# Mixing the first two token tiles side by side, chunk by chunk, with three tiles of token weights turned between them

## The chip, the cores and the metric

The kernel runs on one core of a Trainium2 chip. Its time is the device time of one execution in microseconds (us). Several executions are made, and the median counts. One further execution is taken by the hardware profiler; its times carry line numbers (L419 is line 419 of the kernel before). Engines are called PE (matmul), PEld (its weight load), DVE (vector), ACT (scalar), POOL (GpSimd) and SP (which issues DMAs here).

## The reference

Two blocks follow each other, for a batch of 4, 8 heads, 768 tokens (S) and a head size of 64 (so 512 channels):

```python
scores = scale * q @ k.T + bias            # bias falls off with distance, one slope per head
keep   = is_global | is_local              # 8 global keys, and the last 96 positions
x      = softmax(where(keep, scores, -1e9)) @ v      # -> [B, S, 512]

theta = x @ w_theta
zr, zi = x * cos(theta), x * sin(theta)
y = einsum('ts,bsd->btd', w_tok_r, zr) + einsum('ts,bsd->btd', w_tok_i, zi)
u = x + y
out = u + maximum(u @ w_ch, 0)
```

Inputs and output are float32; the kernel computes in bf16 with float32 sums.

## The kernel before, in words

Tokens are cut into 6 tiles of 128 (NT), channels into 4 (NC), heads into 4 pairs (NP). The loop runs over the batches `b` = 0 to 3. For each batch there are these steps, each a small function:

- **Preparation** (`prep`, batches 1 and 2): DVE copies a head pair's queries and keys into `qkn` (L231, two copies a pair), PE turns them (L246), DVE copies the turned queries to `qT` (L250) and ACT the turned keys to `kT` (L252); `kglob` makes `kG` from `kT` with two DVE copies (L220, L222). Batch 3 is turned by DMA transposes instead (`prep_dma`, L263).
- **Scores** (`scores`): a pair `p` has three chunks `c`. Matmuls go into a wide PSUM buffer `pb` (L296), ACT takes the exponential into `e` (L306), DVE multiplies with a table (L315, L318).
- **Values** (`values`, L355): `e` times `vn` into a wide PSUM buffer; DVE divides by the row sums (`rec`, L364) into `x_sb` (L366). From batch 1 on, `xtrans` turns `x_sb` into `xT` by a DMA transpose that SP issues (L370).
- **Theta** (`theta`, L398): `xT` times `w_theta` in three chunks `c` of two token tiles; ACT takes cosine and sine into `cs` (L404), DVE multiplies with `x_sb` into `zri` (L408). `theta(b, c, 1)` and `(b, c, 3)` complete a chunk and issue its sines.
- **Mix** (`mix(b, tt, g)`, L419): output tile `tt` gets 12 matmuls, 4 for each chunk `g` of two source tiles (cosine and sine part by turns), into one small PSUM tile; after the last, DVE adds `x_sb` to give `u` (L424).
- **`trans_w(tt)`** turns the two token weight matrices for output tile `tt`: 6 PE transposes each into a small PSUM tile (L167), one copy each into `w_tokT` (L168). The copy of the second can be given to ACT. This is done once, for batch 0.
- **`utrans`** turns `u` into `uT` (PE and an ACT copy, L437 and L438, for batch 0; a DMA transpose, L433, afterwards), and **`chan`** multiplies it with `w_ch` (L447), adds and stores (L452, L454).

PSUM has two pools: `big`, two buffers of two banks each (tag `pb`, for scores, for values from batch 1 on, and for theta's first two chunks), and `small`, four buffers (tag `ps`, for all else).

The order has two regimes. All of batch 0 up to its last sine is written out by hand and kept as written (`manual_schedule`); there theta's chunk 0, 1 and 2 are followed by nothing but the tables of `bias_table(1..7)` on ACT. After that a scheduler orders the instructions of each engine ahead of time, and each engine then runs its list in order. What it is given is a list that `weave` makes: `main` (the mixes of batch `b`, with `trans_w`, `chan` and `utrans` among them) and `side` (the attention of batch `b + 1` and preparations), each step with a weight; `weave` spreads `side` between a start share and 0.9 of `main`. For batch 0 the start share is 0.3. Some instructions are fixed behind others (`behind`, `issue_after`).

Loads go over POOL's queue in program order: after the first pieces of batch 0 come the weights, then queries and keys of batch 1, `vn` of batch 1, queries and keys of batch 2, `vn` of batch 2 (its buffer is set by a DVE memset first, L68), half of the queries and keys of batch 3 (L82, into the buffer of batch 1's, so behind the `qkn` copies). The rest of batch 3's loads stand behind `gate` (L469), a one-element POOL copy from `xT` of batch 1, pair 3.

The old order of the mix, and of the weights in `main`:

```python
        for st in (2 * g, 2 * g + 1):
            for wi in range(2):
                anchor["pe"] = nc.tensor.matmul(
...
                if b == 0 and g == 1 and tt + 1 < NT:
                    main.append((1536, lambda tt=tt: trans_w(tt + 1, nc.scalar.copy if tt > 1 else nc.vector.tensor_copy)))
```

Of the kernel before, what the change touches and what calls it, by code (L numbers as in the profile page):

```python
# [9 lines left out]
FP = mybir.dt.float32  # L10
BF = mybir.dt.bfloat16
AF = mybir.ActivationFunctionType
# [4 lines left out]
def kernel(  # L17
# [13 lines left out]
    nc = tc.nc  # L31
    B, H, S, D = q.shape
    T = 128
    NT = S // T
    DM = H * D
    NC = DM // T
    NP = H // 2
# [11 lines left out]
    moe = ctx.enter_context(tc.tile_pool(name="moe", bufs=2))  # L49
    big = ctx.enter_context(tc.tile_pool(name="big", bufs=2, space=bass.MemoryType.PSUM))  # L50
    small = ctx.enter_context(tc.tile_pool(name="small", bufs=4, space=bass.MemoryType.PSUM))

    def ps_big():
        return big.tile([T, 2, 512], FP, name="pb", tag="pb")

    def ps_small(shape, dtype):
        return small.tile(shape, dtype, name="ps", tag="ps")
# [40 lines left out]
    for i_, eng in ((1, nc.sync), (0, nc.scalar)):  # L98
        eng.dma_start(out=qk32[:, i_].rearrange("p h t d -> p h (t d)"),
                      in_=(q, k)[i_][0, 0:2].rearrange("h (p t) d -> p h (t d)", p=T))  # L100
# [39 lines left out]
    def bias_table(h):  # L140
        nc.scalar.activation(etab[:, h], dist[:, 0:5], AF.Exp, scale=-slopes[h])

    halfpi = const.tile([T, 1], FP)
# [7 lines left out]
    w_tokT = [const.tile([T, NT, S], BF, name=f"w_tokT_{wi}") for wi in range(2)]  # L151
# [8 lines left out]
                w_nat[wi, tt], w_nat[wi, tt + 1] = w2[:, 0], w2[:, 1]  # L160
        nc.gpsimd.dma_start(out=w_ch_bf, in_=moe_w_ch.rearrange("(c p) n -> p c n", p=T))

    def trans_w(tt, copy=nc.vector.tensor_copy):
        for wi in range(2):
            ps = ps_small([T, NT, T], BF)
            for st in range(NT):
                nc.tensor.transpose(ps[:, st, :], w_nat[wi, tt][:, st * T:(st + 1) * T], ident)  # L167
            (copy if wi else nc.vector.tensor_copy)(out=w_tokT[wi][:, :, tt * T:(tt + 1) * T], in_=ps)  # L168


# [6 lines left out]
    x_sb, xT_sb = {}, {}  # L177
# [203 lines left out]
    zri, u_sb, uTs, pss, css = {}, {}, {}, {}, {}  # L381

    def theta(b, c, j):
        last0 = [(j_, NC - 1) for j_ in range(2)]
        part = {0: [(0, dc) for dc in range(NC - 1)],
                1: [(1, dc) for dc in range(NC - 1)] + last0,
                2: [(j_, dc) for j_ in range(2) for dc in range(NC - 1)],
                3: last0}[j]
        if c == 0 and j in (0, 2):
            zri[b] = moe.tile([T, 2, NT, DM], BF, name="zri", tag="zri", bufs=1)  # L390
        xT, xb = xT_sb[b], x_sb[b]
        last = c == NT // 2 - 1
        if j in (0, 2):
            pss["th", c] = [ps_small([T, DM], FP) for _ in range(2)] if last else ps_big()
        pb = pss["th", c]
        st = lambda j_: slice((2 * c + j_) * T, (2 * c + j_ + 1) * T)
        for j_, dc in part:
            nc.tensor.matmul(pb[j_] if last else pb[:, j_, :], lhsT=xT[:, dc, st(j_)],  # L398
                             rhs=w_theta_bf[:, dc, :], start=(dc == 0), stop=(dc == NC - 1))
        if j in (1, 3):  # L400
            cs = moe.tile([T, 2, 2, DM], BF, name="cs")
            for i_, bias in ((0, {"bias": halfpi}), (1, {})):
                for o, p_ in [(cs[:, i_, j_], pb[j_]) for j_ in range(2)] if last else [(cs[:, i_], pb)]:
                    nc.scalar.activation(o, p_, AF.Sin, **bias)  # L404
            n = 2 if b else 1
            for i_ in range(2):
                for j_ in range(0, 2, n):
                    nc.vector.tensor_mul(  # L408
                        zri[b][:, i_, 2 * c + j_:2 * c + j_ + n, :].rearrange("p j (g d) -> p j g d", g=NP),
                        xb[:, :, 2 * c + j_:2 * c + j_ + n, :].rearrange("p g j d -> p j g d"),  # L410
                        cs[:, i_, j_:j_ + n].rearrange("p j (g d) -> p j g d", g=NP))

    def mix(b, tt, g):
        if g == 0:
            pss["mix"] = ps_small([T, DM], FP)
        ps = pss["mix"]
        for st in (2 * g, 2 * g + 1):
            for wi in range(2):
                anchor["pe"] = nc.tensor.matmul(  # L419
                    ps, lhsT=w_tokT[wi][:, st, tt * T:(tt + 1) * T], rhs=zri[b][:, wi, st, :],  # L420
                    start=(st == 0 and wi == 0), stop=(st == NT - 1 and wi == 1)).ins
        if g == NT // 2 - 1:
            u_sb[b, tt] = moe.tile([T, DM], BF, name="u", bufs=6)
            anchor["dve"] = nc.vector.tensor_add(  # L424
                u_sb[b, tt].rearrange("p (g d) -> p g d", g=NP), x_sb[b][:, :, tt, :],
                ps.rearrange("p (g d) -> p g d", g=NP)).ins

    def utrans(b, tt):
        u = u_sb[b, tt]
        uT = moe.tile([T, NC, T], BF, name="uT", bufs=5)  # L430
        uTs[(b, tt)] = uT
        if (b or b) and (b, tt) != (B - 1, NT - 1):
            anchor["sp"] = nc.sync.dma_start_transpose(out=uT, in_=u).ins  # L433
            return
        ps = ps_small([T, NC, T], BF)
        for dc in range(NC):
            nc.tensor.transpose(ps[:, dc, :], u[:, dc * T:(dc + 1) * T], ident)  # L437
        nc.scalar.copy(out=uT, in_=ps)  # L438
# [29 lines left out]
    def load_behind(b, tile):  # L468
        g = nc.gpsimd.tensor_copy(out=gate, in_=tile).ins  # L469
        with tc.issue_after(g):  # L470
            load_qk_tokens(b, H // 2, H // 2)
            load_all_v(b)
# [30 lines left out]
    def weave(main, side, s0=0.0, s1=1.0):  # L503

        total = float(sum(w for w, _ in main)) or 1.0
        stot = float(sum(w for w, _ in side)) or 1.0
        done, sdone, i_ = 0.0, 0.0, 0
        for w, f in main:
            f()
            done += w  # L510
            while i_ < len(side) and s0 + (s1 - s0) * (sdone + side[i_][0] / 2) / stot <= done / total:
                side[i_][1]()
                sdone += side[i_][0]
                i_ += 1
        while i_ < len(side):
            side[i_][1]()
            i_ += 1
# [6 lines left out]
    dve, act = nc.vector.tensor_copy, nc.scalar.copy  # L524
# [49 lines left out]
    p = NP - 1  # L574
# [16 lines left out]
    theta(0, 1, 2)  # L591
    xtrans(0, p, dve, 4, 6)
    theta(0, 0, 3)
    theta(0, 1, 3)
    theta(0, 2, 2)
    theta(0, 2, 3)
    for h in range(1, H):
        bias_table(h)
    manual.close()
    for eng in (mybir.EngineType.PE, mybir.EngineType.DVE, mybir.EngineType.Activation):  # L600
        last = [i for i in nc.cur_bb.bb.instructions if i.engine == eng][-1]
        fences.enter_context(tc.issue_after(last))
    rest = []
    for b in range(B):
        nxt = b + 1 if b + 1 < B else None
        lag = 3
        th = [lambda c=c, j=j: theta(b, c, j) for c in range(NT // 2) for j in range(2)]
        pre = [lambda p=p: prep(1, p) for p in range(NP)] if b == 0 else []
        ahead = [[lambda p=p: prep(2, p) for p in range(NP // 2)], [lambda p=p: prep_dma(3, p) for p in range(1)],
                 [], []][b]  # L610
        order = rest[:1] + th[:4] + rest[1:2] + th[4:] + rest[2:] if b else []
        if b == 2:
            order[:0] = [lambda p=p: prep_dma(3, p) for p in range(1, NP)]
        if b == 1:
            order.insert(0, lambda: load_behind(3, xT_sb[1][0:1, NC - 1, 0:1]))
        for f in order:
            f()
        main = []
        for tt in range(NT):
            for g in range(NT // 2):  # L620
                if (b, tt) != (B - 1, NT - 1):
                    main.append((2048, lambda tt=tt, g=g: mix(b, tt, g)))
                if b == 0 and g == 1 and tt + 1 < NT:
                    main.append((1536, lambda tt=tt: trans_w(tt + 1, nc.scalar.copy if tt > 1 else nc.vector.tensor_copy)))
                if tt >= lag and g == 0 and (b, tt) != (B - 1, NT - 1):
                    main.append((2048, lambda tt=tt: chan(b, tt - lag)))
                if b == 0 and tt and g == 1:
                    main.append((512, lambda tt=tt: utrans(b, tt - 1)))
            if b and (b, tt) != (B - 1, NT - 1):
                main.append((0, lambda tt=tt: utrans(b, tt)))  # L630
        side = [(1536, f) for f in pre]
        if b == 0:
            side[:0] = [(0, lambda: load_all_v(2))]
            side.append((0, lambda: (alloc_qk(3), load_qk_tokens(3, 0, H // 2))))
        side += attention_steps(nxt, ahead) if nxt else []
        weave(main, side, 0.3 if b == 0 else 0.0, 0.9)
        rest = [lambda tt=tt, b=b: chan(b, tt) for tt in range(NT - lag, NT)]
        if b == 0:
            rest.insert(1, lambda b=b: utrans(b, NT - 1))
# [44 lines left out]
```

The softmax here doesn't subtract the row's maximum and nothing guards it: scores larger than these inputs give would overflow.

## Time and profile before

| what | value |
|---|---|
| median of 6 executions | 174.73 us (174.38 to 175.68) |
| profiled execution | 174.81 us, span of its instructions 172.9 us |
| PE busy | 159.8 us (92%) |
| DVE busy | 124.5 us (72%) |
| ACT busy | 101.3 us (59%) |
| mixing matmuls, L419 | 68.6 us busy for 271 seen |
| copies into `w_tokT` by DVE and ACT, mean of one | 0.53 and 0.79 us |
| queries of batch 1 (768 KB), issue to landing | 20.55 us, +17.7 |
| keys of batch 1 (768 KB), issue to landing | 22.40 us, +19.7 |

How to read it: busy time is the sum over an engine's instructions, and overlapping ones count once. Matmuls are pipelined, so a matmul's own duration (379 ns for 512 columns) is longer than the step from one to the next. In a timeline each row has start, length, engine, line, operation, output and inputs, count, and in brackets the idle time ahead of it with what ended it. In the chain of waits each row is a start, a length and what the time went to. In a table of windows each row is a stretch, its length, and the busy time of each engine in it with the number of instructions.

### The profile page before, as it was taken

How to read it: one execution, taken by the hardware profiler on the slowest of the kernel's cores; microseconds unless marked ns; L12 is line 12 of the kernel's file. 1: busy time of each engine (PE TensorE's matmuls, PEld its weight loads, DVE VectorE, ACT ScalarE, POOL GpSimd, SP SyncE). 2: the span in 40 equal slices, each digit the busy share in tenths (PEclk: the TensorE clock that was granted, in tenths of full speed). 3: DMA queues.
4: the chain of work that ended last, by engine and by line, in shares of the span. 5: the costliest groups of instructions: out<-in, count | busy, mean ns of one | idle time of the engine just before them, and what ended most of it. 6: DMA issues, size and time to landing. Idle time of an engine off the chain costs nothing.

```text
span 172.9 us, 3709 instructions
## 1 busy us (share of the span) xinstructions
PE 159.8 (92%) x1510; PEld 84.5 (49%) x1534; DVE 124.5 (72%) x265; ACT 101.3 (59%) x130; POOL 40.0 (23%) x45
## 2 busy tenths in 40 slices
PE   7599989889999999999997999999999999999991
PEld 2345556445755565445553464443554644444440
DVE  5635977587999999777996687397876865624442
ACT  4678783999697596199944370789446408500010
POOL 8965446005094110299100000000000000000000
PEclk9969999999999999999999999999999999999999
DMA  5999999999999999899999476779244383324335
GB/s 153 199 171 179 207 210 207 206 204 173 159 205 175 171 133 192 146 112 159 168 136 113 123 169 121 140 147 259 54 90 122 94 156 103 121 42 105 100 91 182
DMA packets 75088, 25.93 MB, mean 150 GB/s; under 512 B 63168, under 2 KB 72128, under 8 KB 75072
## 3 DMA queue, kind: packets, MB, share of 16 engines
q0 software_dynamic: 45680, 12.45, 77.7%
q1 hardware_dynamic: 28976, 12.72, 34.2%
q10 hardware_dynamic: 416, 0.52, 0.9%
q8 instruction: 12, 0.20, 0.5%
q14 instruction: 4, 0.03, 0.0%
HBM read 25.69 MB, written 6.29 MB: 185 GB/s over the span
## 4 chain that ended last, share of the span: by engine, by line
PE 49%; DMA 26%; DVE 12%; POOL 5%; ACT 4%; issue 2%; DVEq 0%; SPq 0%; POOLq 0%
PE ps L419 25%; DMA qk<-in_k_dram 11%; PE ps L447 10%; DMA w_nat<-in_moe_w_tok_r_dram 7%; DMA uT<-u 5%; PE pb L398 4%; PE pb L355 4%; PE pb L296 3%; POOL qk L73 3%; DVE qT L250 2%; PE ps L398 2%; DMA kT<-qk 2%; ACT e L306 2%; DVE o_sb L452 2%; POOL vn L88 2%
## 5 line engine op out<-in xcount | busy, mean ns | idle before, releaser
L419 PE MATMUL ps<-zri,w_tokT 128*128 128x512 bf16 x271 | 68.6, 379 | 2.4 <-DVE zri L408 0.8
L306 ACT ACTIVATE e<-pb 128x1024 bf16<-128x1024 f32 (+1 forms) x48 | 43.7, 960 | 19.4 <-PE pb L296 18.8
L419 PEld LDWEIGHTS <-w_tokT 128*128 128x128 bf16 x288 | 26.0, 98 | 29.8 <-issue 2.1
L424 DVE TENSOR_TENSOR u<-x_sb,ps 128x512 bf16<-128x512 bf16 x24 | 16.4, 684 | 13.3 <-PE ps L419 13.3
L447 PE MATMUL ps<-w_ch_bf,uT 128*128 128x512 bf16 (+1 forms) x98 | 24.2, 371 | 1.3 <-DMA uT<-u 1.2
L408 DVE TENSOR_TENSOR zri<-x_sb,cs 128x1024 bf16<-128x1024 bf16 (+1 forms) x30 | 16.8, 582 | 5.7 <-ACT cs L404 5.5
L404 ACT ACTIVATE cs<-pb,halfpi 128x1024 bf16<-128x1024 f32 x8 | 8.9, 1115 | 19.0 <-PE pb L398 19.0
L452 DVE SCALAR_TENSOR_TENSOR o_sb<-ps,u 128x512 f32<-128x512 f32 (+1 forms) x25 | 16.4, 664 | 4.6 <-PE ps L447 4.6
L296 PE MATMUL pb<-qT,kT 64*128 64x128 bf16 x224 | 15.4, 222 | 2.0 <-DVE qT L211 1.3
L315 DVE TENSOR_TENSOR e<-e,etab 128x1024 bf16<-128x1024 bf16 (+1 forms) x24 | 14.8, 620 | 2.3 <-ACT e L306 2.3
L296 PEld LDWEIGHTS <-kT 64*128 64x128 bf16 x224 | 8.8, 95 | 15.2 <-issue 11.8
L438 ACT COPY uT<-ps 128x512 bf16<-128x512 bf16 x7 | 4.1, 587 | 20.6 <-PE ps L437 20.6
L398 PE MATMUL pb<-w_theta_bf,xT 128*128 128x512 bf16 x62 | 14.7, 379 | 0.1
L355 PEld LDWEIGHTS <-e 128*128 128x128 bf16 x352 | 12.9, 97 | 3.8 <-issue 1.6
L447 PEld LDWEIGHTS <-uT 128*128 128x128 bf16 x100 | 9.1, 98 | 11.5 <-DMA uT<-u 1.7
L398 PEld LDWEIGHTS <-xT 128*128 128x128 bf16 x96 | 9.0, 98 | 10.6 <-DMA xT<-x_sb 0.7
L88 POOL DMA_DIRECT2D vn<-in_v_dram x5 | 9.6, 1927 | 12.1 <-DVE vn L68 10.5
L296 PE MATMUL pb<-qT,kG 64*128 64x128 bf16 x128 | 11.9, 221 | 0.3 <-DVE kG L222 0.2
L366 DVE TENSOR_TENSOR x_sb<-pb,rec 128x768 bf16<-128x768 f32 x12 | 11.4, 954 | 0.4
L82 POOL DMA_DIRECT2D qk<-in_q_dram x8 | 8.5, 1063 | 8.1 <-DVE qkn L231 5.5
L355 PE MATMUL pb<-vn,e 128*128 128x65 bf16 x168 | 9.9, 193 | 0.2 <-ACT e L306 0.2
L318 DVE TENSOR_TENSOR e<-e,etab 128x1024 bf16<-128x1024 bf16 x12 | 8.3, 688 | 2.4 <-ACT e L306 2.4
(73 smaller groups left out, 204.8 us busy)
## 6 DMA issues: line engine op xcount, KB each, us to landing
out_dram<-o_sb SPq DMA_DIRECT2D x23, 256.0 KB, 2.3
vn<-in_v_dram POOLq DMA_DIRECT2D x3, 768.0 KB, 23.4
qk<-in_q_dram POOLq DMA_DIRECT2D x2, 768.0 KB, 21.4
qk<-in_k_dram POOLq DMA_DIRECT2D x2, 768.0 KB, 23.7
w_nat<-in_moe_w_tok_r_dram POOLq DMA_DIRECT2D x3, 384.0 KB, 15.0
w_nat<-in_moe_w_tok_i_dram POOLq DMA_DIRECT2D x3, 384.0 KB, 14.0
vn<-in_v_dram POOLq DMA_DIRECT2D x2, 384.0 KB, 10.2
qk<-in_q_dram POOLq DMA_DIRECT2D x8, 96.0 KB, 10.0
```

The costliest lines, as they stand in the source:

```text
L88: nc.gpsimd.dma_start(out=vn[:, h0:h0 + n, :, 0:D].rearrange("p h t d -> p (h t) d"), in_=v[b, h0:h0 + n].rearrange("h (t p) d -> p (h t) ...
L296: nc.tensor.matmul(pb[:, hh, o:o + T], lhsT=lhsT, rhs=qT[R, (own, nxt)[part]], start=bool(b), stop=bool(b) or (jt == NT - 1 or (j == 1 and ...
L306: ins = nc.scalar.activation(e_c, pb[:, :, 0:n], AF.Exp, scale=scale).ins
L315: nc.vector.tensor_mul(e_c, e_c, tab[:, :, s0:s0 + n // T].rearrange("p a s n -> p a (s n)"))
L355: nc.tensor.matmul(o, lhsT=l_, rhs=r_, start=(i_ == 0), stop=(i_ == len(mms) - 1))
L366: nc.vector.tensor_mul(xv, po4[:, :, :, 0:D], rec.to_broadcast([T, n, nt, D]))
L398: nc.tensor.matmul(pb[j_] if last else pb[:, j_, :], lhsT=xT[:, dc, st(j_)], rhs=w_theta_bf[:, dc, :], start=(dc == 0), stop=(dc == NC - 1))
L408: nc.vector.tensor_mul(zri[b][:, i_, 2 * c + j_:2 * c + j_ + n, :].rearrange("p j (g d) -> p j g d", g=NP), xb[:, :, 2 * c + j_:2 * c + j_ ...
L419: anchor["pe"] = nc.tensor.matmul(ps, lhsT=w_tokT[wi][:, st, tt * T:(tt + 1) * T], rhs=zri[b][:, wi, st, :], start=(st == 0 and wi == 0), ...
L424: anchor["dve"] = nc.vector.tensor_add(u_sb[b, tt].rearrange("p (g d) -> p g d", g=NP), x_sb[b][:, :, tt, :], ps.rearrange("p (g d) -> p g ...
L447: nc.tensor.matmul(ps_c, lhsT=uT[:, dc, :], rhs=w_ch_bf[:, dc, i_ * n:(i_ + 1) * n], start=(dc == 0), stop=(dc == NC - 1))
L452: nc.vector.scalar_tensor_tensor(o_sb[:, cols], in0=ps_c, scalar=0.0, in1=u[:, cols], op0=ALU.max, op1=ALU.add)
```

## The change

The sines become a function of their own, so that they can be issued apart from the last matmuls of a chunk. In the part that is written out by hand, the mixes of output tiles 0 and 1 are now issued too, chunk by chunk for both tiles, and the token weights of tiles 1, 2 and 3 are turned between them, in the wide PSUM buffers (`wide=True`: both halves in one buffer, all transposes ahead of both copies, and both copies on DVE). `main` for batch 0 then has tiles 2 to 5 only, `trans_w(4)` and `(5)` go with tiles 2 and 3 and copy with DVE alone, `utrans(0)` comes after the first matmuls of tile 2, and `side` starts at a share of 0.1 in place of 0.3. In a mix, the four matmuls of a chunk go cosine, cosine, sine, sine, for all batches.

```diff
-    def trans_w(tt, copy=nc.vector.tensor_copy):
-        for wi in range(2):
-            ps = ps_small([T, NT, T], BF)
+    def trans_w(tt, copy=nc.vector.tensor_copy, wide=False):
+        pb = big.tile([T, 2, 2 * 512], BF, name="pbw", tag="pb") if wide else None
+        tiles = [pb[:, wi, 0:S].rearrange("p (t n) -> p t n", t=NT) if wide else ps_small([T, NT, T], BF)
+                 for wi in range(2)]
+        for wi, ps in enumerate(tiles):
             for st in range(NT):
                 nc.tensor.transpose(ps[:, st, :], w_nat[wi, tt][:, st * T:(st + 1) * T], ident)
+            if not wide:
+                (copy if wi else nc.vector.tensor_copy)(out=w_tokT[wi][:, :, tt * T:(tt + 1) * T], in_=ps)
+        for wi, ps in enumerate(tiles if wide else ()):
             (copy if wi else nc.vector.tensor_copy)(out=w_tokT[wi][:, :, tt * T:(tt + 1) * T], in_=ps)
...
-        if j in (1, 3):
-            cs = moe.tile([T, 2, 2, DM], BF, name="cs")
...
+        if j == 1:
+            sines(b, c)
+
+    def sines(b, c):
+        pb, xb, last = pss["th", c], x_sb[b], c == NT // 2 - 1
+        cs = moe.tile([T, 2, 2, DM], BF, name="cs")
...
     def mix(b, tt, g):
         if g == 0:
-            pss["mix"] = ps_small([T, DM], FP)
-        ps = pss["mix"]
-        for st in (2 * g, 2 * g + 1):
-            for wi in range(2):
+            pss["mix", tt] = ps_small([T, DM], FP)
+        ps = pss["mix", tt]
+        for wi in range(2):
+            for st in (2 * g, 2 * g + 1):
                 anchor["pe"] = nc.tensor.matmul(
...
     theta(0, 0, 3)
+    sines(0, 0)
     theta(0, 1, 3)
     theta(0, 2, 2)
     theta(0, 2, 3)
+    trans_w(1, dve, True)
+    sines(0, 1)
+    for g in range(NT // 2):
+        for tt in range(2):
+            mix(0, tt, g)
+        if g < 2:
+            trans_w(2 + g, dve, True)
+        if g == 0:
+            sines(0, 2)
     for h in range(1, H):
         bias_table(h)
...
-        for tt in range(NT):
+        for tt in range(0 if b else 2, NT):
             for g in range(NT // 2):
...
-                if b == 0 and g == 1 and tt + 1 < NT:
-                    main.append((1536, lambda tt=tt: trans_w(tt + 1, nc.scalar.copy if tt > 1 else nc.vector.tensor_copy)))
+                if b == 0 and g == 1 and 4 <= tt + 2 < NT:
+                    main.append((1536, lambda tt=tt: trans_w(tt + 2)))
...
-                if b == 0 and tt and g == 1:
+                if b == 0 and g == 1:
                     main.append((512, lambda tt=tt: utrans(b, tt - 1)))
+                if (b, tt, g) == (0, 2, 0):
+                    main.append((512, lambda: utrans(0, 0)))
...
-        weave(main, side, 0.3 if b == 0 else 0.0, 0.9)
+        weave(main, side, 0.1 if b == 0 else 0.0, 0.9)
```

In the orders that result, nothing but the place of instructions and the engine of three copies differs: the same matmuls, transposes, copies and transfers are issued. After theta of batch 1 the two orders differ in a few places only.

More of the change, by code (lines that the diff above doesn't have):

```diff
@@ L399, in theta @@
                              rhs=w_theta_bf[:, dc, :], start=(dc == 0), stop=(dc == NC - 1))
-        if j in (1, 3):
-            cs = moe.tile([T, 2, 2, DM], BF, name="cs")
[L402 to L411, printed above, removed]
+        if j == 1:
[3 more added lines that the diff above has]
+        cs = moe.tile([T, 2, 2, DM], BF, name="cs")
+        for i_, bias in ((0, {"bias": halfpi}), (1, {})):
+            for o, p_ in [(cs[:, i_, j_], pb[j_]) for j_ in range(2)] if last else [(cs[:, i_], pb)]:
+                nc.scalar.activation(o, p_, AF.Sin, **bias)
+        n = 2 if b else 1
+        for i_ in range(2):
+            for j_ in range(0, 2, n):
+                nc.vector.tensor_mul(
+                    zri[b][:, i_, 2 * c + j_:2 * c + j_ + n, :].rearrange("p j (g d) -> p j g d", g=NP),
+                    xb[:, :, 2 * c + j_:2 * c + j_ + n, :].rearrange("p g j d -> p j g d"),
+                    cs[:, i_, j_:j_ + n].rearrange("p j (g d) -> p j g d", g=NP))
     def mix(b, tt, g):
         if g == 0:
-            pss["mix"] = ps_small([T, DM], FP)
-        ps = pss["mix"]
-        for st in (2 * g, 2 * g + 1):
-            for wi in range(2):
+            pss["mix", tt] = ps_small([T, DM], FP)
+        ps = pss["mix", tt]
+        for wi in range(2):
+            for st in (2 * g, 2 * g + 1):
                 anchor["pe"] = nc.tensor.matmul(
```

## The prediction

> **What bounds the kernel now.** The page comes first. PE is busy for 92% of the 172.9 us span and DVE for 72%, but that is a mean over stages. So the second view is the table of windows around the change (30 to 72 us):
>
> ```profile
> core 0: us, PE busy (x) PEld busy (x) DVE busy (x) ACT busy (x) POOL busy (x), PEclk, DMA share, GB/s
> 30.00:34.00 4.00, 3.85 (x23) 1.92 (x22) 2.32 (x7) 3.64 (x4) 0.00 (x0) 1.00 1.26 206
> 34.00:38.00 4.00, 3.12 (x20) 1.42 (x20) 3.67 (x10) 3.97 (x7) 0.00 (x0) 1.00 1.32 204
> 42.16:56.40 14.24, 13.64 (x174) 8.74 (x177) 14.24 (x34) 11.59 (x17) 6.67 (x7) 1.00 2.17 178
> 42.16:64.77 22.61, 21.69 (x295) 14.01 (x301) 22.54 (x51) 18.09 (x24) 7.88 (x8) 1.00 2.24 168
> ```
>
> From 42.16 to 56.40 DVE is busy for 14.24 us of 14.24, and to 64.77 for 22.54 of 22.61. The holes that the change wants to fill lie earlier, in 30 to 38 us, where PE waits for sines and copies. What stands between the two stretches is told by the chain of waits (start, length, what):
>
> ```profile
> 22.40 19.74 DMA qk<-in_k_dram
> 42.14 0.02 issue
> 42.16 0.54 DVE qkn L231 x2
> ...
> 84.64 8.89 DMA uT<-u
> 93.54 0.05 issue
> 93.58 1.04 PE ps L447 x4
> ```
>
> The keys of batch 1 land at 42.14, and DVE's second copy into `qkn` starts with them. That transfer was issued at 22.40 in a stream of about 200 GB/s, so faster front work doesn't bring it forward. The second piece is a transfer too: PE waits until 93.54 for the turned `u` of batch 1. The timelines of SP, POOL, PE and ACT tell what sets it:
>
> ```profile
> 69.36 1.21 SPq L370 DMA_TRANSPOSE xT<-x_sb  x1
> 72.43 0.18 POOL L469 COPY gate<-xT 1x1 bf16<-1x1 bf16 x1 [7.90 <-DMA xT<-x_sb]
> 80.52 2.28 POOL L88 DMA_DIRECT2D vn<-in_v_dram  x1
> 71.52 3.62 PE L398 MATMUL pb<-w_theta_bf,xT 128*128 128x512 bf16 x16
> 73.45 1.11 ACT L404 ACTIVATE cs<-pb,halfpi 128x1024 bf16<-128x1024 f32 x1 [2.87 <-PE pb L398]
> ```
>
> DVE finishes the last `x_sb` of batch 1 (pair 3) at 69.25. SP turns it at 69.36 and it lands by 72.43. That opens POOL's gate: eight loads of queries and keys, then `vn` of batch 3 at 80.52, whose 13.0 us to landing end at 93.5, just when the `uT` asked for at 84.64 lands. The same `xT` is needed by the seventh theta matmul (71.52 + 6 x 0.216 = 72.8, so 0.4 us of slack), and ACT's sines wait for the eighth. So **DVE's arrival at pair 3's `x_sb` sets the pace** of what follows, by two ways.
>
> **The change, part by part.** Unit prices are pieces of the chain, that is, from one start to the next: a 512-column matmul 0.216 (1.73 for 8), a 128-column transpose 0.056 (0.67 for 12), and on DVE `qkn` 0.27, `qT` 0.87, `kG` 0.20 and 0.09, `u` and `o_sb` 0.60, `e` 0.60 or 0.47, `w_tokT` 0.47, `x_sb` 0.87, `rec` 0.14, the two `vG` 0.61 each.
>
> *Front, 30 to 42 us.* I walk the new order. The sines of chunk 0 end at 32.39 and free a wide buffer; 12 transposes for tile 1 end near 33.2. DVE has made `zri` of chunk 0 by 33.2 (its four multiplications start at 31.50 as before), then copies the two weights to 34.3, makes chunk 1 to 35.9 (4 x 0.38), copies tile 2 to 36.9, makes chunk 2 to 38.4, copies tile 3 to 39.4. PE does 8 matmuls (1.73) and 12 transposes (0.67) in each of these rounds and ends tile 1's sum near 40.1. Then `u` twice, to about 40.9. All weights needed had landed (tiles 2 and 3 by 10.70 + 15.2 and 13.84 + 14.0 us). So DVE is through about 0.9 us before the keys land and must wait for them; PE fills the time with 8 matmuls of tile 2 and `utrans(0)`, to about 42.1. Ahead of the first transposes of `qkn` the old order has 29 mixing matmuls and 24 turned weights, the new one 32 and 36: 3 x 0.216 + 12 x 0.056 = **1.3 us of PE work** moves under the DMA wait. The memset of `vn` now stands behind both `u`, so the next `vn` load is issued near 41 instead of 39.49. Its queue still holds 768 KB loads that land at 52.2 and 55.7: I cost that at nothing; without that cover it would be 1.5 us late.
>
> *DVE after 42.16.* `trans_w(4)` and `(5)` now copy both halves on DVE; before, three DVE copies and three ACT copies (0.70 each) were left after 42. So DVE has one copy more, 0.47, and ACT has 2.1 less. I check the prices on the old order first: the 51 DVE instructions up to the last `e` (ends at 64.77) are 11 `qkn`, 5 `qT`, 5 of each `kG`, 2 `vG`, 3 `w_tokT`, 2 `u`, 12 `e`, 2 `rec`, 2 `x_sb`, 2 `o_sb`: 22.5 us, against 22.61 measured. In the new order, laid beside the old one, a copy and a `u` more stand ahead of that `e`: 42.16 + 22.5 + 0.47 + 0.60 = 65.7. From there to the end of pair 3's `x_sb` stand `rec`, `qT`, `x_sb`, `kG`, `o_sb`, `kG`, `rec`, memset and `x_sb`, 3.88: 69.6 at the earliest, where before it was 69.25. (The old order lost 0.6 us here, waiting for an ACT `kT` and for PE, both behind the `w_tokT` copy on ACT at 65.39. That stall goes, and DVE's own work is late next.) So **+0.36 us with DVE never idle**.
>
> *New waits of DVE.* Scores share two wide PSUM buffers with the values; a buffer comes free at `x_sb`. In the old trace the `e` that follows is ready 1.6 us after that: pair 0's `x_sb` ends at 56.36, eight score matmuls start at 56.41, their exponential ends at 57.95; the second time 60.04 and 61.63. The new order puts 1.2 us of other work between (`e`, `o_sb`), then 1.0 (`e`, two `qkn`). DVE would stand idle for 0.4 and 0.6. The whole price is thus +0.36 to +1.36. I take the second gap and leave the first, as a lag of 0.4 anywhere ahead of it closes it: +0.96.
>
> *The order inside a mix* (all `wi` of one kind first) and the later start of batch 1's steps (0.3 to 0.1 of a shorter list) add no instructions; what they move is in the orders that I counted. After theta of batch 1 the two orders hardly differ, so I carry the shift on undiminished: the gate and ACT's sines both follow pair 3's `xT`. PE's 1.3 us turn into a wait at that theta.
>
> *PE busy or DVE busy?* In 42.16 to 64.77 PE shows 21.69 of 22.61, almost as full as DVE. [...]
>
> **Sum.** The profiled execution took 174.81 us (172.9 of span and 1.9 around it). 174.81 + 0.96 = 175.8. The median of the six runs, 174.73, is 0.08 lower: **175.7 us**.
>
> **Rivals.** *PE is the bound after all: faster.* The 1.3 us moved under the DMA wait then reach the end. For it: PE's 92%, and the chain runs over PE from 66.2 to 84. Against it: DVE without a hole from 42.16 to 64.77, more work on it, and the `xT` and `vn` that follow. It decides if pair 3's `x_sb` comes before about 68 us. 174.7 - 1.3 = 173.4.
>
> *DVE keeps full: no change.* The new waits close, since ACT has 2.1 us less to do and gives its exponentials sooner. Then +0.36, of which theta's 0.4 of slack hides all and the gate none: 174.7 to 175.1. Against it: the exponential after a buffer's release is a round trip that idle ACT doesn't shorten.
>
> *The front overruns: slower still.* Weight copies stand ahead of `zri` on DVE. If the three rounds take over 0.9 us longer than I walked (each copy waits for all 12 transposes, each matmul for both copies), DVE reaches the keys late and all above is added: with 0.8 us beyond the slack, 176.5. Before, DVE waited 1.0 us for such transposes once.
>
> That the order is not what the text says is ruled out by the two orders.
>
> **Chances.** Forecast 0.40, DVE full 0.33, PE the bound 0.20, front overruns 0.07. About 0.5% (0.87 us) is what a measurement of this kernel can tell from no change. The forecast's case reaches below that now and then (0.03), and so does PE's gain (0.01). Faster 0.19, same 0.37, slower 0.44. The range takes PE's price and the front's: 173.3 to 176.6.
>
> **What would show it.** Right: DVE idle ahead of 42.1 and its second `qkn` still at 42.1 to 42.2; six `w_tokT` copies before it; DVE full to about 65.5, with holes ahead of an `e` after `x_sb`; the gate over 0.4 us later than 72.43; PE waiting for `xT` at theta; `vn` of batch 3 and `uT` landing late by as much. Wrong: the keys landing at another time than 42.1, pair 3's `x_sb` before 69.2, theta's first matmuls not followed by a wait, or a gate that moves while the PE matmul at 93.58 doesn't.

## The result and the profile after

The changed kernel took **175.55 us** (median of 11 runs, 174.81 to 176.55), the kernel before 174.09 us on the same chip (22 runs, 173.02 to 175.68). The ratio is **1.0091, interval 1.0063 to 1.012**: slower, by about 1.5 us. The profiled execution of after took 175.07 us with a span of 173.2, so the one profiled pair differs by 0.26 us only. Such a pair is too coarse for the total, but its rows say where the time moved.

Two stretches in the table of windows of after (columns: stretch, length, busy time of PE, PEld, DVE, ACT and POOL, granted clock, DMA share, GB/s), then three pieces of its chain of waits (start, length, what):

```profile
30.00:42.00 12.00, 11.89 (x88) 6.63 (x88) 9.29 (x24) 11.56 (x16) 0.36 (x1) 1.00 1.45 198
42.00:70.00 28.00, 24.58 (x325) 15.48 (x327) 27.99 (x58) 18.98 (x25) 8.53 (x9) 1.00 2.14 166
```

```profile
22.49 19.43 DMA qk<-in_k_dram
...
41.94 2.60 DVE qkn L236 x3
44.53 0.87 DVE qT L255
```

The front went as walked: PE is busy for 11.89 of the 12 us to 42 (10.98 before), and the keys still land when they did (22.49 + 19.43 = 41.92). From 42 to 70 DVE is busy for 27.99 of 28.00. But the chain has a new piece: three `qkn` copies take 2.60 us. The timelines of DVE, POOL and PE of after say why (start, length, engine, line, operation, count, idle time ahead of it):

```profile
38.15 1.02 DVE L173 COPY w_tokT<-pbw 128x768 bf16<-128x768 bf16 x2
39.09 1.48 DVE L433 TENSOR_TENSOR u<-x_sb,ps 128x512 bf16<-128x512 bf16 x2
40.53 0.44 DVE L236 COPY qkn<-qk 128x768 bf16<-128x768 bf16 x1
40.69 0.10 DVE L68 MEMSET vn<- 128x48 bf16 x1
41.94 2.07 DVE L236 COPY qkn<-qk 128x768 bf16<-128x768 bf16 x1 [0.96 <-DMA qk<-in_k_dram]
```

```profile
41.64 2.21 POOL L88 DMA_DIRECT2D vn<-in_v_dram  x1 [12.50 <-DVE qkn L236]
```

```profile
44.06 0.51 PE L251 MATMUL ps<-ident,qkn 128*128 128x128 bf16 x6 [1.94 <-DVE qkn L236]
```

DVE idles 0.96 us ahead of the keys, as predicted. Then **the first copy of the keys takes 2.07 us, where the mean of such copies before is 0.35**. It lies under POOL's issue of the next `vn` load and ends 0.16 us after it (41.64 + 2.21 = 43.85; 41.94 + 2.07 = 44.01). Before, the same POOL issue lay beside copies of weights out of PSUM and a `u`, which kept their length. These are the rows of POOL and DVE before, and the group of `qkn` copies from 42 to 70 us (line, count, busy time, mean in ns, idle time ahead):

```profile
39.49 2.21 POOL L88 DMA_DIRECT2D vn<-in_v_dram  x1 [10.53 <-DVE vn L68]
39.69 1.02 DVE L168 COPY w_tokT<-ps 128x768 bf16<-128x768 bf16 x2 [1.04 <-PE ps L167]
41.11 0.69 DVE L424 TENSOR_TENSOR u<-x_sb,ps 128x512 bf16<-128x512 bf16 x1 [0.40 <-PE ps L419]
L231 DVE COPY qkn<-qk 128x768 bf16<-128x768 bf16 x12 | 3.9, 350 | 0.1
```

The rows that answer to those of SP, POOL, PE, ACT and PE again before:

```profile
71.64 1.26 SPq L375 DMA_TRANSPOSE xT<-x_sb  x1
74.44 0.70 POOL L478 COPY gate<-xT 1x1 bf16<-1x1 bf16 x1 [11.61 <-DMA xT<-x_sb]
81.56 2.29 POOL L88 DMA_DIRECT2D vn<-in_v_dram  x1
74.44 1.90 PE L403 MATMUL pb<-w_theta_bf,xT 128*128 128x512 bf16 x7 [0.55 <-DMA xT<-x_sb]
75.08 1.11 ACT L413 ACTIVATE cs<-pb,halfpi 128x1024 bf16<-128x1024 f32 x1 [4.03 <-remote]
93.75 1.03 PE L456 MATMUL ps<-w_ch_bf,uT 128*128 128x512 bf16 x4
```

("Remote" in ACT's row stands for a releaser that the profile doesn't name.) Against before, pair 3's `xT` is issued 2.28 us later (69.36), the gate opens 2.01 later (72.43) and the first sine starts 1.63 later (73.45). Yet `vn` of batch 3 is issued only 1.04 later (80.52), and the matmul that before waited for `uT` at 93.58 stands at 93.75, without a wait: **in this pair almost all is given back between 75 and 94**. So two things are to be explained, a loss that I had not priced and a gain that I had denied.

### The profile page after: what moved, and what is told of

Read it like the earlier page. It is cut to its first block, busy times and chain, and to the rows that moved or that the text cites. A ratio compares the mean times of both kernels' runs of the same rounds, so it can differ in the third digit from the quotient of the medians.

```text
span 173.2 us, 3707 instructions
## 1 busy us (share of the span) xinstructions
PE 158.2 (91%) x1510; PEld 84.1 (49%) x1534; DVE 127.5 (74%) x268; ACT 99.3 (57%) x127; POOL 37.9 (22%) x45
## 4 chain that ended last, share of the span: by engine, by line
PE 49%; DMA 21%; DVE 13%; ACT 7%; POOL 5%; another core or an unknown queue 2%; issue 2%; DVEq 0%; SPq 0%; POOLq 0%; ACTq 0%
PE ps L428 27%; DMA qk<-in_k_dram 11%; PE ps L456 8%; DMA w_nat<-in_moe_w_tok_r_dram 7%; PE pb L360 5%; PE pb L301 4%; ACT cs L413 4%; POOL qk L73 3%; DVE qkn L236 2%; DVE qT L255 2%; PE pb L403 2%; DMA kT<-qk 2%; PE ps L251 2%; POOL vn L88 2%
## 5 line engine op out<-in xcount | busy, mean ns | idle before, releaser
L257 ACT COPY kT<-ps 128x768 bf16<-128x768 bf16 x8 | 6.4, 797 | 5.6 <-PE ps L251 5.4
```

## The experiments

The main theory: POOL's issue of the `vn` load, which the moved memset brings under the keys' copies, costs about 1.3 us; the two weight copies moved from ACT to DVE cost the rest. The rivals: the copies alone, the start share of 0.1, or the matmul order. Each ratio below is to the kernel before on the same chip.

**The load alone.** After, with the load of batch 2's `vn` put where DVE still works on the weights. DVE's and PE's lists stay as they are otherwise.

```diff
     theta(0, 2, 3)
+    load_all_v(2)
     trans_w(1, dve, True)
...
-            side[:0] = [(0, lambda: load_all_v(2))]
```

> The changed kernel with the memset of batch 2's vn, and with it POOL's issue of that load, moved from behind both u (40.7 and 41.64 us) to behind chunk 0's zri, near 33 and 34 us. Nothing else moves on DVE or PE. Theory A, on record before (DVE has one copy more and waits for exponentials): the load's place costs nothing, so the ratio to the kernel before stays near 1.009. Theory B, from the trace after: the 2.21 us in which POOL issues the load hold up one qkn copy, 2.07 us in place of 0.35, so 1.7 us of DVE come back, pair 3's x_sb ends near 69.7 in place of 71.5, and the ratio falls to 0.998 to 1.002.

174.42 us, ratio **1.0016 [0.9989, 1.0043]**. POOL's and DVE's timelines of this run:

```profile
38.79 2.21 POOL L88 DMA_DIRECT2D vn<-in_v_dram  x1 [9.30 <-DVE w_tokT L173]
40.08 1.07 DVE L236 COPY qkn<-qk 128x768 bf16<-128x768 bf16 x1
42.27 0.90 DVE L236 COPY qkn<-qk 128x768 bf16<-128x768 bf16 x3 [1.11 <-DMA qk<-in_k_dram]
```

The memset moved to 32.96 as meant, but POOL issued the load only at 38.79, not near 34; what it waited for, these runs don't settle. The issue now meets the copy of the queries, which takes 1.07 us and again ends 0.15 after POOL's (41.00; 41.15). But that copy lies in the wait for the keys, so it costs nothing; the three copies after the landing take 0.90. From the keys' copy to the start of pair 3's `x_sb` there are 26.99 us, in after 28.69: 1.70 less, just the length of the hold. The later load costs 0.75% (1.0091 to 1.0016), 1.3 us. Not all of the 1.70 arrives: SP had a store ahead of pair 3's transpose and issued it at 71.01, 0.78 after the end of that `x_sb`, in after 0.04.

**The copies alone.** After, with the second copy of tiles 4 and 5 on ACT again; the load stays late.

```diff
-                    main.append((1536, lambda tt=tt: trans_w(tt + 2)))
+                    main.append((1536, lambda tt=tt: trans_w(tt + 2, nc.scalar.copy)))
```

> The changed kernel with the second copy of trans_w(4) and trans_w(5) on ACT, as before the change. DVE has 0.94 us less ahead of pair 3's x_sb, ACT 1.4 us more. Theory A: the DVE work is all there is, so about 0.9 us are won and the ratio falls to 1.003 to 1.005. Theory B: the held copy stays, so the same 0.9 us at most; with the copy of tile 5 on ACT among the last exponentials, as in the kernel before, less: 1.004 to 1.009.

174.93 us, ratio **1.0049 [1.0013, 1.0084]**: the two copies are worth 0.42%, 0.7 us; the prediction's price for two was 0.94. The intervals of the two ratios overlap, so this price is less sure than that of the load, whose two intervals don't meet. The hold is still there, on the third copy now. The rows of POOL and DVE:

```profile
41.65 2.43 POOL L88 DMA_DIRECT2D vn<-in_v_dram  x1 [12.96 <-DMA qk<-in_k_dram]
41.61 0.63 DVE L236 COPY qkn<-qk 128x768 bf16<-128x768 bf16 x2 [0.62 <-DMA qk<-in_k_dram]
```

Copies that start 0.04 us before POOL's row (41.61) and 0.23 after it (41.88) run through, and the issue takes 0.22 longer; the third ends at 44.24, 0.16 after the issue.

**The late load in the kernel before.** Nothing of the change, but the memset of `vn` fixed behind tile 1's `u`.

```diff
+    def late_v2():
+        with behind("dve"):
+            alloc_v(2)
+        load_v(2, 0, 8)
...
+            if (b, tt) == (0, 1):
+                main.append((0, late_v2))
...
-            side[:0] = [(0, lambda: load_all_v(2))]
```

> The kernel before with the memset of batch 2's vn held back behind the u of tile 1 (near 41.7 in place of 38.54 us), so that POOL issues the load near 42.6, among the qkn copies. Theory A: the load's data are needed only by batch 2, so nothing changes: 0.999 to 1.001. Theory B: one qkn copy is held until POOL is done near 44.8, 1.5 to 2 us longer, and DVE has no slack to 69 us: 1.006 to 1.011, with nothing of the change in it.

175.57 us, ratio **1.0083 [1.0048, 1.0118]**. The late load makes the old kernel as slow as the new one. A copy is held there too, until 0.15 us after the issue's end:

```profile
43.05 2.21 POOL L88 DMA_DIRECT2D vn<-in_v_dram  x1 [13.44 <-PE ps L246]
44.19 1.22 DVE L231 COPY qkn<-qk 128x768 bf16<-128x768 bf16 x1
```

**Both undone.** The early load and ACT's copies together (the two edits above, on after).

> The changed kernel with both: the vn load issued near 34 us and the second copies of tiles 4 and 5 on ACT. Theory A: as with the ACT copies alone, 1.003 to 1.005. Theory B: 1.7 us of the held copy and 0.5 to 0.9 us of DVE work come back, 0.993 to 0.998, so that the change would pay once its load is out of the way.

173.82 us, ratio **0.9973 [0.9947, 0.9999]**. The two prices add, as far as the intervals can tell: 0.43% between the early load with and without ACT's copies, 0.42% with the late load; 0.75% and 0.76% for the load. What is left of the change is a small gain, and the next run says how far to trust it.

**Before once more.** The kernel before, unchanged, as if it were an experiment.

> The kernel before, unchanged, for a second profile: whether its DMA wait near 93.5 us and the late landing of batch 1's keys (42.14) are there each time. Both theories: ratio 1.000; keys near 42; pair 3's x_sb 27.1 us after the keys; PE's wait for uT near 93 us again, if it is a part of this kernel and not of one execution.

174.05 us, ratio 0.9972 [0.994, 1.0003]. The same code measured 0.3% faster than itself, so a single 0.9973 proves no gain. PE's wait for `uT` is there again (0.94 us, at 92.70). (The repeat of the version above gave 0.9983, below.)

**One more tile turned in the front.** On that version, tile 4's weights too are turned in the wide buffers.

```diff
-        if g < 2:
-            trans_w(2 + g, dve, True)
+        trans_w(2 + g, dve, True)
...
-                if b == 0 and g == 1 and 4 <= tt + 2 < NT:
+                if b == 0 and g == 1 and 5 <= tt + 2 < NT:
```

> On top of the early vn load and the ACT copies: the weights of tile 4 are turned in the hand-written part too, so that two DVE copies (0.94 us) and 12 transposes (0.7 us) fill the time in which DVE and PE wait for batch 1's keys (DVE about 1.1 us). One DVE copy and one ACT copy less after 42 us. Theory B (DVE is the bound there): 0.47 us less than with the two edits alone, 0.993 to 0.996. Rival (PE or the keys' landing sets the end by now): no change, 0.997.

174.38 us, ratio 1.0011 [0.9985, 1.0036], a miss. DVE did reach pair 3's `x_sb` earlier (68.25 against 68.80). But its `xT` landed later: the gate opened at 73.30 against 72.76, and theta waited 1.73 us for it (0.55 in after). Why that transpose took 4.0 us from its issue at 69.31, where others take about 3, was not tried.

**The start share.** The same version, with batch 1's steps spread from a share of 0.3 again.

```diff
-        weave(main, side, 0.1 if b == 0 else 0.0, 0.9)
+        weave(main, side, 0.3 if b == 0 else 0.0, 0.9)
```

> The changed kernel with the early vn load and the ACT copies, and batch 1's steps started at a share of 0.3 in place of 0.1. Theory B: the order of DVE's work before pair 3's x_sb changes by one or two instructions of 0.6 us: 0.995 to 1.003 against 0.9973. Rival: the early start is what lets PE use the front's gain, and without it the stretch gets a hole of 1 us or more: 1.003 to 1.010.

179.16 us, ratio **1.024 [1.0192, 1.0287]**, far from what I expected. Its waits by engine have a new first line for DVE, and its chain a new transfer:

```profile
DVE vG L341 <- DMA vn<-in_v_dram: 2.3, 1, 2.3
```

```profile
24.65 23.19 DMA vn<-in_v_dram
```

DVE's `vG` comes so early in its list that it waits 2.3 us for batch 1's `vn`, with all else behind it. In that execution the granted clock from 42 to 70 us was 0.88 too, so not all of the 2.4% need be the order's; but the fastest execution, with a clock of 0.998 over the whole, took 177.47 us, still 1.9% above before. The share of 0.1 is no cost of the change: with 0.3 this version is slower.

**The old order inside a mix.** The same version, cosine and sine by turns again.

```diff
-        for wi in range(2):
-            for st in (2 * g, 2 * g + 1):
+        for st in (2 * g, 2 * g + 1):
+            for wi in range(2):
```

> The changed kernel with the early vn load and the ACT copies, and cosine and sine matmuls by turns again as in the kernel before. Both theories: the count is the same and the sum is the same; the first mix of each batch waits for a sine product one matmul sooner, at most 0.2 us a batch: 0.996 to 1.001 against 0.9973.

174.05 us, ratio 0.9971 [0.9946, 0.9997]: the same as with the new order (0.9973, 0.9983). These runs show no worth of it.

**What was given back.** The rows of before around 73 us, POOL's and DVE's, and the PE row that waits:

```profile
72.66 2.19 POOL L82 DMA_DIRECT2D qk<-in_q_dram  x1
74.85 0.83 POOL L82 DMA_DIRECT2D qk<-in_k_dram  x1
72.68 0.69 DVE L337 COPY vG<-vn 8x2080 bf16<-8x2080 bf16 x1
73.29 1.15 DVE L231 COPY qkn<-qk 128x768 bf16<-128x768 bf16 x4
93.58 1.04 PE L447 MATMUL ps<-w_ch_bf,uT 128*128 128x512 bf16 x4 [1.24 <-DMA uT<-u]
```

POOL's first load behind the gate takes 2.19 us, the next, of the same size, 0.83. During it DVE runs `vG` and four `qkn` copies back to back, and the load ends 0.4 us after the last. In after the gate opens later, and its first load, at 75.08 when the copies are through, takes 0.82. So in before it is DVE that holds POOL: `vn` of batch 3 is issued 8.1 us after the gate instead of 7.1, `uT` lands late, and PE waits 1.24 us. To test that, these four copies were moved, in the kernel before, to right behind pair 3's `x_sb` and `o_sb`, where DVE idles. Only DVE's list changes.

```diff
-        with behind("dve"):
+        with behind("x" if (b, p // 2) == (2, 1) else "dve"):
...
-        if p == 0 or (b, p) == (2, NP // 2):
+        if p == 0:
             prep_copy(b, p)
-        if p + 1 < NP and (b, p) != (2, NP // 2 - 1):
+        if p + 1 < NP and b != 2 or p == 0:
             prep_copy(b, p + 1)
...
-        nc.vector.tensor_mul(xv, po4[:, :, :, 0:D], rec.to_broadcast([T, n, nt, D]))
+        anchor["x"] = nc.vector.tensor_mul(xv, po4[:, :, :, 0:D], rec.to_broadcast([T, n, nt, D])).ins
...
+        if b == 1:
+            steps.extend((0, lambda p=p: prep_copy(2, p)) for p in (2, 3))
```

> Before, with nothing of the change in it: the four DVE copies qkn of batch 2's pairs 2 and 3 (in before one group at 73.29, 1.15 us) are put behind x_sb of batch 1's pair 3, four operations earlier on DVE, where DVE idles 0.92 us. No other engine's order is touched. Theory A (after theta, before loses about 1.3 us that the change does not lose, because POOL's first gated load of batch 3 is held by these copies: 2.19 us against 0.82 us in after, so that vn of batch 3 is issued, and uT lands, as much later): the first gated load takes about 0.8 us, the load of vn is issued about 7.1 us after the gate in place of 8.1, PE's wait for uT near 93 goes, and the time falls by 0.9 to 1.3 us: ratio 0.992 to 0.995, and first sine to u of the next batch is 31.7 to 31.9 us in place of 33.2. Theory B (these microseconds come from elsewhere, such as the order of the channel tiles after theta): the load becomes short, but first sine to u stays at 32.9 to 33.2 us and the ratio at 0.997 to 1.003.

173.63 us, ratio **0.9962 [0.9939, 0.9985]**. POOL's and PE's rows:

```profile
72.19 0.18 POOL L469 COPY gate<-xT 1x1 bf16<-1x1 bf16 x1 [9.04 <-DMA xT<-x_sb]
72.43 0.82 POOL L82 DMA_DIRECT2D qk<-in_q_dram  x1
79.01 2.28 POOL L88 DMA_DIRECT2D vn<-in_v_dram  x1
92.20 1.03 PE L447 MATMUL ps<-w_ch_bf,uT 128*128 128x512 bf16 x4
```

The load is short, `vn` follows the gate by 6.8 us, and PE's wait is gone. From the first sine (73.47) to the last `u` of batch 1 (105.25) it is 31.78 us, the same as in after (106.80 - 75.08 = 31.72); in before it was 33.19 (106.64 - 73.45), in its repeat 32.90. The gain, 0.7 us by the ratio, is less than these 1.1 to 1.4 of single profiles and than I expected (a ratio of 0.992 to 0.995).

**The same on the changed kernel, and that kernel again.** The version with the early load and ACT's copies, with these four copies moved as above, and without.

> The changed kernel with the early load of v and ScalarE's copies (the version that measured 0.9973), and the same four copies behind x_sb of batch 1's pair 3. There the gated loads were hardly held (the gate itself waited some tenths). Theory A: at most the tenths at the gate to gain: 0.994 to 0.998. Theory B: no difference to that version, 0.995 to 0.999. A time above 1.001 would say that u and the channel tiles that now stand 1.15 us later on DVE are missed.

> The version that measured 0.9973 once more, beside the two others of this call on one chip: 0.995 to 1.000 if that small gain is real; 1.000 or above if it was noise between placements.

173.32 us, ratio **0.9957 [0.9929, 0.9986]**, and 173.76 us, ratio 0.9983 [0.9959, 1.0007]. The first has the shortest time of all, but the three intervals on this chip (0.9962, 0.9957, 0.9983) overlap. With the collisions gone from both, the old arrangement (173.63 us, 0.9962) and the new (173.32 us, 0.9957) differ by 0.1 to 0.3 us, which these runs cannot tell from nothing.

**What the hold is.** After, with one copy, that of the first keys, on ACT.

```diff
-                nc.vector.tensor_copy(
+                (nc.scalar.copy if (b, p, i_) == (1, 0, 1) else nc.vector.tensor_copy)(
```

> After, with one copy alone put on another engine: the copy of batch 1's first keys (qkn of pair 0, held from 41.94 to about 44.0 on DVE while POOL issued its load of vn) runs on ScalarE. DVE's next copy of keys then stands first there under the same issue, so both engines copy the same kind of tile from the same landing, side by side, within 41.9 to 44. The recorded order of the instructions between 42 and 60 shifts with it, so the time is read with care. Theory A (POOL's issue holds VectorE's copies that read and write SBUF, not copies as such): ScalarE's copy takes about 0.8 to 1.1 us and PE's first transposes of these keys start near 43.2 in place of 44.06, while VectorE's first copy of keys is still held to about 44. Since VectorE has no idle time from there to 70, the time hardly gains: 1.004 to 1.010. Theory B (the landing itself is slow, or any engine's access to SBUF is held): ScalarE's copy too ends only near 44. Theory C (PE's wait of 1.94 us for these keys is the price, not VectorE's time): the time falls by over 0.9 us, to 1.000 to 1.004.

174.87 us, ratio 1.0073 [1.0048, 1.0098]. POOL's, ACT's and DVE's rows:

```profile
41.26 2.33 POOL L88 DMA_DIRECT2D vn<-in_v_dram  x1 [12.26 <-DVE qkn L236]
42.30 0.83 ACT L236 COPY qkn<-qk 128x768 bf16<-128x768 bf16 x1
41.39 0.36 DVE L236 COPY qkn<-qk 128x768 bf16<-128x768 bf16 x1 [0.53 <-DMA qk<-in_k_dram]
41.78 0.96 DVE L255 COPY qT<-ps 128x768 bf16<-128x768 bf16 x1
43.79 0.63 DVE L236 COPY qkn<-qk 128x768 bf16<-128x768 bf16 x2 [1.05 <-PE ps L251]
```

ACT's copy takes 0.83 us in the middle of the issue: neither the landing nor copies as such are slow. DVE's copy out of PSUM isn't held either. But theory A failed on its main point: DVE's copy of keys, started 0.13 us after POOL's row, took 0.36. With the rows of the second experiment (0.23 after: free, POOL 0.22 longer) and of after (0.30 after: held) this fits a hold that POOL takes only between 0.23 and 0.30 us into its row, and not while DVE has it. The Trainium skill's "SBUF — State Buffer", section "SBUF: two separate sides", describes a port pair that VectorE's faster copies and GpSimd share as an exclusive lock, held by whichever starts first for the whole instruction, with loads from GpSimd's queue short of descriptors while VectorE has it. These runs show a hold in both directions (a copy of 2.07 us in place of 0.35, and, above, an issue of 2.19 in place of 0.82), and by them the start of the POOL row is not yet the start of the hold. That a port pair is the reason, no run here shows.

Here DVE reached pair 3's `x_sb` 1.31 us sooner than in after, though now it waited 1.05 us for PE. Then a store stood ahead on SP, the transpose was issued 0.82 us after that `x_sb`, and the first sine came only 0.54 sooner (74.54). The run with the early load had its first sine at 74.54 too and measured 1.0016, with an interval that doesn't meet this run's 1.0048 to 1.0098. The two profiles can't explain that: one took 175.05 us, 0.6 above the median of its run, the other 174.51, the shortest of its seven. So the price of the load's place stands on the ratios of the runs with and without it, and how the freed time of DVE reaches the end is only in part traced.

## Why the prediction was right and wrong

The forecast, slower by about 1 us, held in sign and nearly in size (0.97 us forecast, 1.46 measured), but that it came so near is luck: its sum left out a loss of 1.3 us, counted waits of 0.60 that didn't come, and denied a gain. The pieces, each from one profiled execution:

| from the copy of the first keys to the start of pair 3's `x_sb` | us |
|---|---|
| before (42.16 to 68.38) | 26.22 |
| after (41.94 to 70.63) | 28.69 |
| after with the early load (42.27 to 69.26) | 26.99 |
| after with ACT's copies (41.61 to 69.75) | 28.14 |
| after with both (42.38 to 68.80) | 26.42 |

- *What bounds it* was right. DVE from the keys' landing to pair 3's `x_sb` sets the pace; PE's 1.3 us moved forward brought no gain that the runs could show. PE stood idle instead: 0.55 us at theta, which the prediction named, and 1.94 us for the held copy of the keys, which it didn't. The 0.4 us of slack there was right too: the gate moved 2.01 and the first sine 1.63.
- *DVE after 42.16*: the work term, +0.36 with a copy more, was about right (its own prices add up to 22.4 for the 51 instructions, not 22.5, which changes little). Without the hold the stretch is 0.77 longer (26.99 against 26.22); some 0.4 of that is the two `vG` copies, which take 1.01 and 0.78 there and 0.70 and 0.69 in before, with POOL's issues beside them in both.
- *New waits of DVE*, 0.60: wrong. DVE is busy for 28.65 of these 28.69 us in after and for 26.94 of 26.99 with the early load. The round trip from a buffer's release to its exponential did not come to light: the exponentials that I had behind pair 0's `x_sb` started before it ended (58.98 against 58.98 + 0.93 = 59.91).
- *"I cost that at nothing"*, the later `vn` load: **the step that failed**. I looked at the load's landing, which indeed nobody misses, and not at its issue, 2.2 us on POOL, and what runs on DVE beside it. It holds one copy for 1.7 us and costs 0.75%, 1.3 us. In before the same issue stood beside PSUM copies.
- *"I carry the shift on undiminished"*: wrong as well, and the prediction had named the sign, a gate that moves while the PE matmul at 93.58 doesn't. In before the chain from the gate to `uT` held a POOL load stretched by DVE's copies. The later gate let those copies pass first. Moving them in before alone is worth 0.38% (0.7 us).

In ratios: 0.75% for the load and 0.42% for the two copies are what lies between the changed kernel and the version without both. That version measured 0.2 to 0.3% faster than before, no more than before against itself, and the edit that removes the other collision alone, on before, gives 0.4%. So no gain of the side-by-side mixing itself is left that these runs could show. Of the rivals, PE as the bound is refuted by the time (175.55 us, not 173.4) and by pair 3's `x_sb`, which started at 70.63 and not before 68; "DVE keeps full" was right in its mechanism and wrong in its time, since the hold came on top.

## What to carry to other kernels

A load's price has two ends: when it lands, and what runs while POOL issues it. Before moving anything that releases a POOL load, look at which VectorE copies between SBUF tiles then lie under its issue, and put the issue beside waits or work out of PSUM. And a delay is not to be carried to the end unchanged: see whether what it moves stood in a collision before.

## What the runs showed of the hardware

- A 0.35 us copy on DVE from SBUF to SBUF took 2.07, 1.07 and 1.22 us when it met POOL's 2.21 us issue of a 768 KB load, and ended 0.15 to 0.16 us after the issue each time. Copies out of PSUM kept their length (`w_tokT` 1.02 for two, `qT` 0.96), and a copy on ACT in the middle of the issue took 0.83.
- The other way round, POOL's issue of a 96 KB load took 2.19 us in place of 0.82 while DVE ran five copies from SBUF to SBUF back to back (2.32 in the repeat of before).
- On SP a transpose with a store ahead of it was issued 0.8 us after its data were ready in two experiments, 0.04 in after; there the first sine gained 0.54 us where DVE had gained 1.3 to 1.4.
